# Attention and routed experts on one core: the next batch's scale of v five steps later, its loads, maxima and splits later too, z's splits four steps later, and another rate for the weights' work

## The chip, the cores and the metric

The program runs on one core of a Trainium2 chip. TensorE (PE in the profile) multiplies matrices, VectorE (DVE) and ScalarE (ACT) do elementwise work, GpSimd (POOL) issues scattered transfers, SyncE (SP) issues nearly all other transfers. The metric is device time in microseconds (us), the median of the runs of a kernel. Run to run it spreads by some 0.3% (2160.58 to 2166.72 us before the change).

## What is computed

The reference, cut to what matters (B = 8 batches, S = 2496 tokens, D = 256, d_qk = 64; 8 experts with F = 1024):

```python
scores = (1/S) * z @ z.T                    # per batch, S x S
attn   = maximum(scores, 0) ** 2
x      = u * (attn @ v)                     # (B*S, D) rows
xn     = x / norm(x);  en = emb / norm(emb)
idx    = argmax(xn @ en.T / tau);  gate = softmax(...)[idx]
out    = gate * (maximum(x @ w1[idx], 0) @ w2[idx])
```

The kernel multiplies in float16 and keeps float32 precision by halves: it splits every operand into a high and a low float16 part, scaled by a power of two that is found on the chip: for z, v and each expert's weights it takes the largest absolute value, turns it into a power of two, and then writes the two halves.

## The kernel before, in words

**Two phases.** In the first some 1315 us the attention of the 8 batches runs, with the routing of the rows of x and the splitting of the experts' weights beside it; then come the experts' products. The change touches the first phase alone.

**Steps.** The first phase is a loop over 800 steps (line 1085 on): batch b, group g of 512 query tokens (5 groups, 0 to 4; the last has 448), and 20 key tiles of 128 tokens. A step is written here by its number within its batch, 0 to 99, so steps 60 to 79 are group 3 and 80 to 99 the last group. In each step PE does `values` (lines 373 to 393: 12 products, into `acc`). Scores are symmetric: a tile is computed once (`scores`, lines 279 and 280; ACT makes relu and square, lines 283 and 284; `parts` makes high and low halves `hl` on DVE, lines 326 and 327) and for later groups turned by a DMA transpose on SP (lines 340, 342). So only "own" steps compute scores: 20 in group 0, then 16, 12, 8 and 4. In group 3 these are the steps 72 to 79; steps 60 to 71 have `values` alone. `scores` runs three own steps ahead of its use.

**Preparing the next batch.** `ahead(b)` makes a list of (step, flag, work) for batch b + 1, and the loop takes from its head what is due: loads and maxima of z (`scan_load`, `scan_max`), then of v (ten tiles `vr`, line 107; maxima line 121), the scale of z in steps 54 and 58, the scale of v in steps 64 and 68, then the loads (`z_load`, line 181), the splits (`z_split`: ACT line 192, DVE line 195) and copies (`z_copy`) of z. An item whose flag is set waits while `state["pm"]` holds, and with it all behind it in the list.

**A scale** has two pieces (`scale_pieces`). `across` reduces the maxima on DVE (line 132, `smv`), lets PE transpose the column (line 134, into `pm`) and reduces again on DVE (lines 136, 137, 139, `smbv`). `spread` lets PE spread the result over the partitions (line 144, into `pm`) and makes the scale on DVE (lines 146, 148). `pm` is one single buffer (pool `psM`), shared with the rank of the routing and the scales of the weights.

**Routing.** After each group `route` makes a queue of 29 small works, one taken per step. Those of the group before run in the next one: squares on ACT (line 445), a root on DVE (lines 713 to 727), a split of the rows (ACT line 468, DVE line 469) and its DMA transpose (line 472). The rank (lines 524, 525 on PE, into `pm`) comes in step 3 of the next but one group and is read in step 5 (`place`, lines 534, 537, 539, `pos`); between the two `state["pm"]` holds. In the steps of a batch this is 63 to 65, so v's `across` of step 64 runs in step 66.

**Splits of v** (`v_split`, ACT line 243, DVE line 244) are written in the program for steps 78 and 79 (`early = 2`) and 80 to 97. **Weights**: 22 works per expert (`wq`: loads lines 585 and 588, maxima line 596, scales lines 602 to 617, splits lines 645 and 646), one taken whenever `wsum`, which grows by `WRATE` per step, passes 1.

**Order.** PE executes in the order of the program, so a product that waits stops PE. For DVE, ACT and SP a scheduler sets the order when the kernel is built; each then executes in that order.

Of the kernel before, what the change touches and what calls it, by code (L numbers as in the profile page):

```python
# [43 lines left out]
def relu2_attention_then_moe(ctx, tc, zT, u, v, emb, tau, w1, w2, ident, tri, iota_e, out):  # L44
# [40 lines left out]
    NVP = NST // 2  # L85
# [17 lines left out]
    def scan_load(b, what, i, eng=None):  # L103

        if what == "v":
            t = vring.tile([P, 2, D], F32, name="vr", tag="vv")
            (eng or nc.sync).dma_start(t, v[b, 2 * i * P:2 * (i + 1) * P, :].rearrange("(j p) d -> p j d", p=P))
            for j in range(2):
                vraw[b, 2 * i + j] = t[:, j, :]
            scan[b, what, i] = t.rearrange("p j d -> p (j d)")  # L110
            return
        t = wk.tile([P, SCAN], F32, name="scan", tag="scan", bufs=1)
        src = zT[b, i * (DQ // ZSCANS):(i + 1) * (DQ // ZSCANS), :]
        (eng or nc.sync).dma_start(t, src.rearrange("a c -> (a c)").rearrange("(p w) -> p w", p=P))
        scan[b, what, i] = t

    def scan_max(b, what, i):
        if i == 0:
            n = (NVP if b else NV0) if what == "v" else ZSCANS if b else 3
            scan[b, what] = sml.tile([P, n], F32, name="smx" + what)  # L120
        nc.vector.tensor_reduce(scan[b, what][:, i:i + 1], scan.pop((b, what, i)), axis=AX.X, op=ALU.max,
                                apply_absolute_value=True)
# [48 lines left out]
    def z_tiles(b):  # L171
        Zs[b] = (zpool.tile([P, SP], F16, name="z1", tag="z1"),
                 zpool.tile([P, SP], F16, name="z2", tag="z2"))
# [3 lines left out]
    def z_load(b, c0):  # L177
        zt = zpool.tile([P, ZC], F32, name="zt", tag="zt", bufs=3)
        c1 = min(c0 + ZC, SP)
        m = P if b == 0 else DQ  # L180
        nc.sync.dma_start(zt[:m, :c1 - c0], zT[b, :m, c0:c1])
        zraw[b, c0] = zt

    def z_split(b, c0):
        zt = zraw.pop((b, c0))
        w = min(ZC, SP - c0)
        c1 = c0 + w
        z1, z2 = Zs[b]
        c = slice(c0, c1)
        lo, hi = slice(0, DQ), slice(DQ, P)  # L190
        k = scan[b, "cz"]
        hi_ = nc.scalar.activation(z1[lo, c], zt[lo, :w], AF.Copy, scale=k[lo]).ins
        if b == 0:
            nc.scalar.activation(z2[hi, c], zt[hi, :w], AF.Copy, scale=k[hi])
        lo_ = nc.vector.scalar_tensor_tensor(z2[lo, c], zt[lo, :w], k[lo], z1[lo, c], op0=ALU.mult, op1=ALU.subtract).ins
        if b:
            state["as"], state["ds"] = hi_, lo_
        if b == 0:
            nc.vector.scalar_tensor_tensor(z1[hi, c], zt[hi, :w], k[hi], z2[hi, c], op0=ALU.mult, op1=ALU.subtract)  # L199

    def z_copy(b, c0, c1):
        z1, z2 = Zs[b]
        c = slice(c0, c1)
        nc.sync.dma_start(z1[DQ:P, c], z2[0:DQ, c])
        nc.sync.dma_start(z2[DQ:P, c], z1[0:DQ, c])
# [549 lines left out]
    accs = {}  # L755
    wq = [f for e in range(E) for f in weights(e)]
    wsum = 0.0
    WRATE = {False: (0.0, 0.18, 0.22, 0.37, 0.33), True: (0.2, 0.3, 0.3, 0.35, 0.35)}

# [283 lines left out]


    NB = NG * NST
    early = 2

    def ahead(b):  # L1050

        todo = []
        for i in range(ZSCANS):
            todo.append((16 + 8 * i, False, lambda i=i: scan_load(b + 1, "z", i)))
            todo.append((23 + 8 * i, False, lambda i=i: scan_max(b + 1, "z", i)))
        for i in range(NVP):
            todo.append((3 * i + 25, False, lambda i=i: scan_load(b + 1, "v", i)))
            todo.append((3 * i + 34, False, lambda i=i: scan_max(b + 1, "v", i)))
        at = {"z": 54, "v": 3 * NVP + 34}
        for k, what in enumerate("zv"):  # L1060
            for j, f in enumerate(scale_pieces(b + 1, what)):
                todo.append((at[what] + 4 * j, True, f))
        at = 64
        gap = 2
        todo.append((0, False, lambda: z_tiles(b + 1)))
        for k in range(ZN):
            todo.append((max(0, at + (k - 3) * gap), False, lambda k=k: z_load(b + 1, k * ZC)))
            todo.append((at + k * gap, False, lambda k=k: z_split(b + 1, k * ZC)))
            if k in (ZN // 2, ZN - 1):
                c0, c1 = (0, (k + 1) * ZC) if k == ZN // 2 else ((ZN // 2 + 1) * ZC, SP)  # L1070
                todo.append((at + k * gap, False, lambda c0=c0, c1=c1: z_copy(b + 1, c0, c1)))
        return sorted(todo, key=lambda x: x[0])

    todo = []
    nd = 0
    for i, (b, g, q, s) in enumerate(steps):
# [10 lines left out]
        if q == 0:  # L1087
            accs[b, g] = [psA.tile([P, 512], F32, name=f"acc{k}", tag=f"a{2 * ((b * NG + g) % 2) + k}") for k in range(2)]
            nx = (b, g + 1) if g + 1 < NG else (b + 1, 0)
            upiece = None  # L1090
            if nx[0] < B:
                uts[nx], upiece = u_load(*nx)
            if g == 0 and b + 1 < B:
                todo = ahead(b)
# [51 lines left out]
        if i >= NST + 6:  # L1146
            wsum += WRATE[b == B - 1][g]
        if wsum >= 1 and not state["pm"]:
# [116 lines left out]
```

## Time and profile before

| | before |
|---|---|
| runs, us | 2160.58, 2164.53, 2166.72 (median 2164.53) |
| the profiled execution, us | 2163.31 |
| its span in the trace, us | 2161.7 |
| granted TensorE clock, mean | 0.992 |
| PE / DVE / ACT busy, us | 2102.2 / 1326.1 / 1026.0 |

A span is the time from the first to the last instruction in the trace; the profiled execution's own time has 1.6 us more. PE is busy 97% of the span, so what can be won without taking products away lies in PE's waits and in the clock that it is granted. The views used below are: who waited for whom, busy time by stretch, and the instructions in order of time.

### The profile page before, as it was taken

What the parts mean: (1) busy time and instruction counts of PE and PEld (TensorE: products, weight loads), DVE (VectorE), ACT (ScalarE), POOL (GpSimd) and SP (SyncE); (2) the same over time, 40 slices, a digit from 0 to 9 for tenths busy, and PEclk for the clock granted to TensorE, in tenths of its full rate; (3) what the DMA queues carried; (4) which work ended last, traced back from release to release, by engine and by line L of the source; (5) the groups of instructions that cost most, each with busy time, mean ns of one, the idle gap of its engine ahead of it and who ended that gap; (6) DMA issues with size and microseconds to landing.
All of it is one profiled execution on the core that took longest, in us unless ns stands there. A gap on an engine that the chain in (4) does not pass through costs nothing. (4 is left out here: it accounts for less than half of the span.)

```text
span 2161.7 us, 50676 instructions
## 1 busy us (share of the span) xinstructions
PE 2102.2 (97%) x19210; PEld 1789.3 (83%) x19210; DVE 1326.1 (61%) x4005; ACT 1026.0 (47%) x2131; POOL 328.5 (15%) x344
## 2 busy tenths in 40 slices
PE   6999999999999999999999999999999999999998
PEld 4878878878878878878778888888888888888888
DVE  8787787787787787787787874433333333333333
ACT  7676666566666566666566652222222222222211
POOL 0011011011011011011011102211211111211111
PEclk9999999999999999999999999999999999999999
DMA  6977977977977987977987968433323332257474
GB/s 160 193 157 157 195 164 153 192 169 150 205 162 152 188 176 152 199 165 153 197 166 165 184 134 205 124 71 89 92 55 92 89 89 50 50 135 198 131 201 115
DMA packets 661832, 317.60 MB, mean 147 GB/s; under 512 B 562885, under 2 KB 639310, under 8 KB 655440
## 3 DMA queue, kind: packets, MB, share of 16 engines
q1 hardware_dynamic: 646112, 272.76, 59.9%
q0 software_dynamic: 15184, 41.24, 6.9%
q8 instruction: 152, 2.49, 0.5%
q14 instruction: 96, 0.79, 0.1%
q10 hardware_dynamic: 288, 0.33, 0.1%
HBM read 255.11 MB, written 59.60 MB: 146 GB/s over the span
## 5 line engine op out<-in xcount | busy, mean ns | idle before, releaser
L283 ACT ACTIVATE a<-sc 128x512 f32<-128x512 f32 (+1 forms) x480 | 269.7, 562 | 271.7 <-PE sc L280 208.8
L548 POOL DMA_INDIRECT xs<-row,dsti x160 | 168.2, 1051 | 1016.0 <-ACT a L283 442.2
L284 ACT ACTIVATE a<-a 128x512 f32<-128x512 f32 (+1 forms) x480 | 285.9, 596 | 11.2
L384 PE MATMUL acc<-vv,tt 128*128 128x256 f16 x1152 | 273.9, 276 | 0.0
L386 PE MATMUL acc<-vv,tt 128*128 128x256 f16 x1152 | 273.7, 276 | 0.0
L1011 POOL DMA_INDIRECT out_dram<-ot,me x159 | 154.6, 972 | 662.5 <-DVE ot L1010 638.6
L1006 PE MATMUL po<-w,hl 128*128 128x256 f16 x928 | 252.9, 273 | 0.0
L1004 PE MATMUL po<-w,hh 128*128 128x256 f16 x928 | 252.9, 273 | 0.0
L1005 PE MATMUL po<-w,hh 128*128 128x256 f16 x928 | 252.9, 273 | 0.0
L1010 DVE TENSOR_SCALAR ot<-po,me,w 128x256 f32<-128x256 f32 x116 | 58.3, 540 | 216.4 <-PE po L1006 212.5
L388 PE MATMUL acc<-vv,tt 128*128 128x256 f16 x1152 | 181.2, 276 | 0.0
L279 PE MATMUL sc<-z 128*128 128x512 f16 (+1 forms) x480 | 175.8, 366 | 4.2 <-DVE z L199 4.1
L280 PE MATMUL sc<-z,z 128*128 128x512 f16 (+1 forms) x480 | 175.8, 366 | 0.0
L1006 PEld LDWEIGHTS <-hl 128*128 128x128 f16 x1272 | 124.5, 98 | 14.4
L1005 PEld LDWEIGHTS <-hh 128*128 128x128 f16 x1272 | 124.5, 98 | 14.2
L1004 PEld LDWEIGHTS <-hh 128*128 128x128 f16 x1272 | 124.5, 98 | 14.2
L388 PEld LDWEIGHTS <-tt 128*128 128x128 f16 x1152 | 114.1, 99 | 14.3
L386 PEld LDWEIGHTS <-tt 128*128 128x128 f16 x1152 | 114.1, 99 | 14.0
L384 PEld LDWEIGHTS <-tt 128*128 128x128 f16 x1152 | 113.9, 99 | 14.1
L468 ACT ACTIVATE row<-x,up 128x256 f16<-128x256 f32 x160 | 70.9, 497 | 69.4 <-DVE up L456 64.4
L1004 PE MATMUL po<-wb,hh 128*128 128x256 f16 x344 | 93.8, 273 | 0.0
L1005 PE MATMUL po<-wb,hh 128*128 128x256 f16 x344 | 93.8, 273 | 0.0
(5250 smaller groups left out, 5493.9 us busy)
## 6 DMA issues: line engine op xcount, KB each, us to landing
w<-wsd SPq DMA_DIRECT2D x64, 1026.0 KB
wa<-wsd SPq DMA_DIRECT2D x46, 1024.0 KB
w<-wsd SPq DMA_DIRECT2D x42, 1024.0 KB
wb<-wsd SPq DMA_DIRECT2D x24, 1026.0 KB
ut<-in_u_dram SPq DMA_DIRECT2D x72, 256.0 KB
vr<-in_v_dram SPq DMA_DIRECT2D x70, 256.0 KB
wr<-in_w_dram SPq DMA_DIRECT2D x64, 256.0 KB
wsd<-wo SPq DMA_DIRECT2D x64, 256.0 KB
```

The costliest lines, as they stand in the source:

```text
L279: nc.tensor.matmul(sc[:, :n], z1[:, ss], z1[:, t0:t0 + n], start=True, stop=False)
L280: nc.tensor.matmul(sc[:, :n], z1[:, ss], z2[:, t0:t0 + n], start=False, stop=True)
L283: state["at"] = nc.scalar.activation(a[:, :n], sc[:, :n], AF.Relu, scale=2.0 ** -SHIFT).ins
L284: nc.scalar.activation(a[:, :n], a[:, :n], AF.Square)
L384: nc.tensor.matmul(outs[j], piece(ph, j), vh, start=first and j % 2 == 0, stop=False, skip_group_check=True)
L386: nc.tensor.matmul(outs[j], piece(ph, j), vl, start=False, stop=False, skip_group_check=True)
L388: nc.tensor.matmul(outs[j], piece(pl, j), vl if last else vh, start=False, stop=ends, skip_group_check=True)
L548: put = nc.gpsimd.indirect_dma_start(xs[:, :], bass.IndirectOffsetOnAxis(ap=loc["dsti"][:m, j:j + 1], axis=0), row[:m, j, :], None)
L1004: nc.tensor.matmul(o, hh[:, f, t], wh, start=(f == 0), stop=False)
L1005: nc.tensor.matmul(o, hh[:, f, t], wl, start=False, stop=False)
L1006: nc.tensor.matmul(o, hl[:, f, t], wh, start=False, stop=(f == NF - 1))
L1011: put = nc.gpsimd.indirect_dma_start(out, bass.IndirectOffsetOnAxis(ap=me.bitcast(U32)[:, j, 1:2], axis=0), ot[:, j, :], None, bounds_chec ...
```

## The change

Seven numbers change. The scale of v goes from steps 64 and 68 (in effect 66 and 68) to 71 and 75. The loads of v go from steps 25 to 52 to 28 to 55, its maxima from 34 to 61 to 37 to 64. The splits of z go from 64 to 82 to 68 to 86, with their loads (58 to 76 to 62 to 80) and copies (74 and 82 to 78 and 86). The splits of v are written for steps 80 to 99. The weights' rates by group change from 0, 0.18, 0.22, 0.37, 0.33 to 0.05, 0.2, 0.28, 0.28, 0.29 (both 22 works in 100 steps). No instruction is added or removed.

```diff
-    WRATE = {False: (0.0, 0.18, 0.22, 0.37, 0.33), True: (0.2, 0.3, 0.3, 0.35, 0.35)}
+    WRATE = {False: (0.05, 0.2, 0.28, 0.28, 0.29), True: (0.2, 0.3, 0.3, 0.35, 0.35)}
...
-    early = 2
+    early = 0
...
-            todo.append((3 * i + 25, False, lambda i=i: scan_load(b + 1, "v", i)))
-            todo.append((3 * i + 34, False, lambda i=i: scan_max(b + 1, "v", i)))
-        at = {"z": 54, "v": 3 * NVP + 34}
+            todo.append((3 * i + 28, False, lambda i=i: scan_load(b + 1, "v", i)))
+            todo.append((3 * i + 37, False, lambda i=i: scan_max(b + 1, "v", i)))
+        at = {"z": 54, "v": 3 * NVP + 41}
...
-        at = 64
+        at = 68
```

**ACT, batch 1, from the end of group 2 to step 72.** Before the change ACT's order is (`a` relu and square of scores, `sq` the routing's squares, `row` its row splits, `z_2878` a split of z, `vv` a split of v):

```order
L507 ACTIVATE ex<-sh 128x32
L283 ACTIVATE a<-sc 128x512
L192 ACTIVATE z_2878<-zt,scz 64x256
L284 ACTIVATE a<-a 128x512
L445 ACTIVATE sq,n_4495<-x 128x256 x4
L192 ACTIVATE z_2878<-zt,scz 64x256
L468 ACTIVATE row_100<-x,up 128x256 x2
L192 ACTIVATE z_2878<-zt,scz 64x256
L468 ACTIVATE row_100<-x,up 128x256 x2
L192 ACTIVATE z_2878<-zt,scz 64x256
L243 ACTIVATE vv<-vr,scv 128x256 x15
L283 ACTIVATE a<-sc 128x512
```

After the change, the same place:

```order
L507 ACTIVATE ex<-sh 128x32
L283 ACTIVATE a<-sc 128x512
L284 ACTIVATE a<-a 128x512
L445 ACTIVATE sq,n_4496<-x 128x256 x4
L192 ACTIVATE z_2875<-zt,scz 64x256
L468 ACTIVATE row_100<-x,up 128x256 x3
L192 ACTIVATE z_2875<-zt,scz 64x256
L468 ACTIVATE row_100<-x,up 128x256
L283 ACTIVATE a<-sc 128x512
```

The first split of z now stands behind the four squares instead of ahead of them, and the run of 15 splits of v ahead of step 72's scores is gone.

**ACT, batch 1, steps 75 to 78, after the change.** Here the splits of v now begin, two at a time between the scores' works:

```order
L284 ACTIVATE a<-a 128x256
L243 ACTIVATE vv<-vr,scv 128x256 x2
L283 ACTIVATE a<-sc 128x256
L192 ACTIVATE z_2875<-zt,scz 64x256
L284 ACTIVATE a<-a 128x256
L243 ACTIVATE vv<-vr,scv 128x256 x2
L239 ACTIVATE vh<-vr,scv 64x256
L283 ACTIVATE a<-sc 128x448
```

Six of the 20 splits stand ahead of the end of group 3, the other 14 in the last group.

**DVE, batch 1, the second half of v's `across`.** Before (`smbv` is what PE's spread waits for; `z_2879` the low half of z, `row_100` of a row, `mx` a weights' maximum):

```order
L195 SCALAR_TENSOR_TENSOR z_2879<-zt,scz,z_2878 64x256
L724 SCALAR_TENSOR_TENSOR xy<-xt_4636,xy 128x4
L469 SCALAR_TENSOR_TENSOR row_100<-x,up,row_100 128x256
L727 TENSOR_TENSOR xs<-xn2c,xy 128x4
L596 TENSOR_REDUCE mx<-wr_3760 128x1
L136 TENSOR_REDUCE sm1v<-pm 1x1
L460 TENSOR_SCALAR inv<-xs,ceps 128x4
L137 TENSOR_SCALAR sm1v<-sm1v 1x1
L461 RECIPROCAL inv<-inv 128x4
L139 TENSOR_SCALAR smbv<-sm1v 1x1
```

After:

```order
L727 TENSOR_TENSOR xs<-xn2c,xy 128x4
L460 TENSOR_SCALAR inv<-xs,ceps 128x4
L461 RECIPROCAL inv<-inv 128x4
L462 SCALAR_TENSOR_TENSOR inv<-inv,itau,dn 128x4
L136 TENSOR_REDUCE sm1v<-pm 1x1
L137 TENSOR_SCALAR sm1v<-sm1v 1x1
L139 TENSOR_SCALAR smbv<-sm1v 1x1
L195 SCALAR_TENSOR_TENSOR z_2876<-zt,scz,z_2875 64x256
L326 CAST hl__4786<-a 128x4x128
L326 CAST hl__4809<-a 128x4x128
```

The chain from `pm` to `smbv` now stands behind the whole root of the routing and ahead of the first halves `hl` of group 3's own steps.

## Rows read from the trace of the kernel before

**Rows 1.** The page: span, and busy time, share and instructions of each engine.
```profile
span 2161.7 us, 50676 instructions
PE 2102.2 (97%) x19210; PEld 1789.3 (83%) x19210; DVE 1326.1 (61%) x4005; ACT 1026.0 (47%) x2131; POOL 328.5 (15%) x344
```
**Rows 2.** Waits of PE, 100 to 1160 us: who, for whom; us, times, longest.
```profile
PE pm L134 <- DVE pos L539: 12.7, 6, 3.3
PE pm L144 <- DVE smbv L139: 7.9, 5, 1.9
PE acc L384 <- DVE hl__16713 L326: 1.7, 1, 1.7
...
PE acc L384 <- DVE hl__15359 L326: 0.4, 1, 0.4
...
PE acc L384 <- DVE hl__2239 L326: 0.4, 1, 0.4
```
**Rows 3.** Busy time by stretch: batch 1's groups 2, 3, 4; batch 7's group 3.
```profile
core 0: us, PE busy (x) PEld busy (x) DVE busy (x) ACT busy (x) POOL busy (x), PEclk, DMA share, GB/s
255.00:287.00 32.00, 32.00 (x289) 26.36 (x287) 26.49 (x91) 17.77 (x39) 4.35 (x4) 1.00 1.06 231
...
287.00:324.00 37.00, 33.36 (x281) 26.91 (x280) 29.53 (x110) 23.91 (x60) 4.21 (x5) 0.91 0.60 132
...
324.00:351.00 27.00, 27.00 (x255) 23.19 (x253) 17.12 (x69) 12.79 (x29) 4.67 (x5) 1.00 0.61 132
...
1260.00:1289.00 29.00, 29.00 (x274) 25.04 (x272) 18.70 (x64) 16.07 (x38) 3.89 (x4) 1.00 0.73 160
```
**Rows 4.** The same view, stretches behind v's scale, batches 1, 2, 3, 6.
```profile
298.00:306.00 8.00, 7.29 (x40) 5.34 (x41) 6.01 (x30) 2.63 (x8) 3.90 (x4) 0.59 0.71 186
462.00:470.00 8.00, 7.46 (x41) 5.40 (x42) 5.91 (x31) 2.53 (x7) 3.88 (x4) 0.60 0.66 173
622.00:633.00 11.00, 8.24 (x58) 6.58 (x59) 9.92 (x42) 6.56 (x17) 3.89 (x4) 0.84 0.68 169
...
1108.00:1118.00 10.00, 7.71 (x53) 6.09 (x54) 8.96 (x38) 5.73 (x15) 3.89 (x4) 0.83 0.61 159
```
**Rows 5.** PE in order of time, batch 1: start, us, instruction [idle before <-releaser].
```profile
293.62 0.60 PE L388 MATMUL acc<-vv,tt 128*128 128x256 f16 x4
...
294.93 0.60 PE L388 MATMUL acc<-vv,tt 128*128 128x256 f16 x4
298.71 0.37 PE L134 MATMUL pm<-idt,smv 128*1 128x128 f32 x1 [3.19 <-DVE pos L539]
...
300.58 1.06 PE L388 MATMUL acc<-vv,tt 128*128 128x256 f16 x4
```
**Rows 6.** SP's issues in order of time, batch 1.
```profile
289.74 0.58 SPq L181 DMA_DIRECT2D zt<-in_zT_dram  x1
290.43 1.22 SPq L342 DMA_TRANSPOSE joint<-hl__4462  x1
```
**Rows 7.** ACT in order of time, batch 1.
```profile
291.94 0.51 ACT L192 ACTIVATE z<-zt,scz 64x256 f16<-64x256 f32 x1 [4.95 <-DMA zt<-in_zT_dram]
...
297.16 0.91 ACT L468 ACTIVATE row<-x,up 128x256 f16<-128x256 f32 x2 [1.30 <-DVE up L456]
...
305.14 6.11 ACT L243 ACTIVATE vv<-vr,scv 128x256 f16<-128x256 f32 x15 [5.00 <-DVE scv L148]
```
**Rows 8.** DVE in order of time, batch 1.
```profile
295.01 0.17 DVE L713 TENSOR_SCALAR xn2c<-n 128x4 f32<-128x4 f32 x1 [4.46 <-ACT sq L445]
295.09 0.68 DVE L596 TENSOR_REDUCE mx<-wr 128x1 f32<-128x512 f32 x1
...
298.53 0.19 DVE L539 TENSOR_TENSOR pos<-pos,ob 128x32 f32<-128x32 f32 x1
```
**Rows 9.** Waits of ACT, 100 to 1160 us.
```profile
ACT z L192 <- DMA zt<-in_zT_dram: 35.5, 21, 5.2
```
**Rows 10.** PE in order of time, batch 0: the spread of z's scale, step 58.
```profile
125.14 0.38 PE L144 MATMUL pm<-smbz,ones_f 1*128 1x1 f32 x2
```

## The prediction

> **What bounds the kernel now.** I read the page first: PE is busy 2102.2 of 2161.7 us [rows 1], so the change can win only what PE waits or what it runs at the lower clock. Next the waits of PE between 100 and 1160 us, which leave out the start and batch 7. Two lines stand out, and both belong to the scale of v: the transpose (line 134) waits 12.7 us in six batches, for `pos`, the last step of the routing's `place`; the spread (line 144) waits 7.9 us in five, for `smbv` [rows 2]. The other lines are waits of `values` for a half `hl`, 0.4 to 1.7 us each. Then the busy time by stretch: group 3 of batch 1, where v's scale is made, takes 37 us at a mean clock of 0.91; group 3 of batch 7, where no next batch is prepared, 29 us at 1.00 [rows 3]. So the place to look at is group 3 of batches 0 to 6.
>
> **Why PE waits there.** Three rows of batch 1 give the chain. ACT stands idle 4.95 us until 291.94, for the load of z's first piece [rows 7], which SP issued only at 289.74 [rows 6]; by ACT's order the routing's squares stand behind that split. DVE waits 4.46 us for the squares and begins the root at 295.01 [rows 8]. `pos` stands on DVE behind two splits of z, most of the root and two weights' maxima and ends at 298.7 [rows 8]. PE came to the transpose at 295.5 (the step's last products begin at 294.93 and last 0.60) and waits 3.19 us [rows 5]. It isn't a case of batch 1 alone: ACT waits 35.5 us for z's loads, 21 times [rows 9].
>
> Behind such a wait PE gets the lower clock: the same four products take 0.60 us before it and 1.06 us after it [rows 5]. The granted clock shows 0.59 of 8 us, 0.60 of 8, 0.84 of 11 and 0.83 of 10 in four batches [rows 4], that is 1.2 instead of 2.4 GHz for a part of each stretch. At 1.00 as much work would take 8 x 0.41 + 8 x 0.40 + 11 x 0.16 + 10 x 0.17 = 9.9 us less.
>
> The Trainium skill (TensorE: Matmul & The Clock Gate, Part 1, the caveats on the trace of the clock gate) says that recorded clock events are not to be trusted singly and should be checked against what the matmuls cost; were the records wrong, the 9.9 us would not be there to be won and the sum below would end at 2142. The doubled 1.06 us [rows 5] decides for the records.
>
> **The change part by part.**
>
> *v's scale to steps 71 and 75.* What goes: 12.7 + 7.9 + 9.9 = 30.5 us, if PE finds `pos` and `smbv` ready. For the transpose: it moves from two steps behind the rank to seven behind it. A step without scores takes 1.31 us (293.62 to 294.93 [rows 5]); without the wait PE in batch 1 would start step 66 at 295.5 and come to the new place at 295.5 + 5 x 1.31 = 302.0. `pos` is ready earlier, an estimate from rows: the squares no longer stand behind z's first split, but the load of that split now stands behind two turns `joint` on SP (1.22 each [rows 6]) and is issued near 293; it took 2.2 us from issue to ACT (289.74 to 291.94 [rows 6, 7]), so the split runs near 295.2, then three row splits at about 0.45 (0.91 for two [rows 7]), then `pos`: about 298. Cover: 4 us. If that cover is gone, each us late costs 1 us per batch and perhaps the clock again. For the spread: it follows four steps later, about 6 us with scores in three of them. DVE's chain lines 136 to 139 stands behind nothing that is still open once the root is done, so it needs 1 us of these 6. What stays: the instructions themselves. What they cost beside full work is seen with z's scale, whose spread runs in 0.38 us with no wait ahead of it [rows 10]; between 100 and 1160 us no wait of z's scale is in the list at all [rows 2]. I take 30.5, the whole; the bounds are 30.5 and half of it, 15 (below).
>
> Who waits behind the moved instructions: on DVE the reads of the spread (lines 146, 148) now stand between the halves `hl` of steps 75 and 76, and behind them ACT's first split of v, behind that the scores of step 76. No wait of this kind at this place is in the trace. Its nearest rows: the waits of `values` for `hl`, 0.4 to 1.7 us [rows 2]; so 0 to 7 x 1.7 = 12 us. I take 0, as z's scale, likewise among own steps (12 in group 2), has none [rows 2], and as `values` begins with the high half alone.
>
> *v's splits (`early` 0).* The order shows the real move: a run of 15 splits that keeps ACT from 305.14 to 311.25 [rows 7], ahead of step 72's scores, dissolves into pairs, and 14 go to the last group. The late start behind that run leaves five waits of 0.4 us for `hl` (first and last of them in rows 2): 2.0 us, of which I take 1. In the last group 14 x 0.41 (6.11 / 15 [rows 7]) = 5.7 us are added to ACT and about as much to DVE, which have 27 - 12.79 = 14.2 and 27 - 17.12 = 9.9 us to spare there [rows 3], and 16 of its 20 steps need nothing of them. Cost nothing; without that cover PE would wait in the last four steps.
>
> *z's splits, loads and copies four steps later.* Four splits then lie in the last group instead of two: 1 us more on either engine, in the same spare time. The first use is the next batch's scores in step 97; the second copy moves from step 82 to 86, 11 steps or some 14 us ahead. Nothing.
>
> *v's loads and maxima three steps later.* On SP they pass some of the rows' turns and of the weights' loads; the last maximum is due in step 64, seven steps or 9 us ahead of the scale. Nothing.
>
> *The weights' rate.* 22 works per batch before and after. Group 2 gets 1.2 more, at 0.68 us for a maximum [rows 8]: 0.8 us on a DVE with 26.49 busy of 32 [rows 3]. Group 3 gets 1.8 fewer. Group 2 is where DVE has least room: at worst one wait like the 1.7 [rows 2] in every batch, 12 us; at best group 1's and 2's waits go, some 6 us. I take nothing.
>
> **The sum.** Against the profiled execution: 2163.3 - 30.5 - 1 = 2131.8, rounded 2132 us. The median of the runs before is 1.2 us above that execution, well inside their spread of 6 us; I give 2132 for the median after.
>
> **The rivals.**
>
> *The wait comes along.* `pos` or `smbv` is still late in steps 71 and 75, since the load of z that ACT waits for comes later too. For it: the same chain, with 35.5 us of such waits [rows 9], and only 4 us of cover. Against it: five more steps, and the squares first. Half of the 30.5 stays: 2147 (2139 to 2155).
>
> *The scores' chain pays.* In steps 73 to 79 DVE and ACT must serve scores, z's splits, v's scale and v's first splits at once, without the time that PE's waits gave them: group 3 shrinks from 37 to near 31 us with 29.5 us of DVE work in it [rows 3]. If every batch waits 1.7 us [rows 2] in two or three steps, 4.4 us in all, the gain is gone: 2163.
>
> *Slower: v's splits hold up the hand-over.* A split's buffer is free only once PE has left an older tile of v in the last group; on ACT, behind the waiting split, stand z's last split, the row splits and the relus of step 96 on. DVE spares 9.9 us there, of which the added 5.7 and 1.0 leave 3.2. To end above 2170 the hand-over must cost (2170 - 2132) / 7 = 5.4 us per batch, so these queues must stand still 8.6 us; with 9.6 the time is 2177. Against it: PE leaves those tiles in steps 82 to 86, ten steps ahead of 96.
>
> *More than the sum.* Group 1's and 2's waits go as well: 2126.
>
> That the change doesn't do what it says is excluded by the orders shown.
>
> **How the numbers follow.** Forecast 2132 (2128 to 2138): 0.73. The wait comes along: 0.13. More: 0.05. The scores' chain pays: 0.05. Slower: 0.04. For faster by over 0.3% (6.5 us, about what a measurement of this kernel can tell from no change) count the first three: 0.91; same 0.05, slower 0.04. The range takes the forecast, the better case down to 2125 and the rival's nearer half up to 2145.
>
> **What would show it.** Right: in the waits of PE between 100 and 1130 us the lines `pm L134 <- pos` and `pm L144 <- smbv` are gone or under 1 us in all; the clock is 1.00 through group 3 of every batch; group 3 of batch 1 takes about 31.5 us; ACT's squares run ahead of its wait for z. Wrong: `pm L134` waits under another name (`smv`, `pos`), or `acc L384 <- hl` grows by more than 5 us, in group 3 for the scores' chain, at the end of group 4 for the hand-over. The forecast fails above all if z's first load lands over 4 us later than I worked out.

## The result, and the profile after

The changed kernel takes 2133.9 us (median; 2132.47 to 2135.95) against 2162.56 us for the kernel before in the same comparison, a ratio of 0.9873 with a 95% interval of 0.9859 to 0.9888. The forecast was 2132, its range 2125 to 2145. The profiled execution has 2132.47 us and this page:

```profile
span 2130.9 us, 50630 instructions
...
PE 2091.0 (98%) x19210; PEld 1785.8 (84%) x19210; DVE 1316.9 (62%) x4005; ACT 1024.0 (48%) x2131; POOL 376.5 (18%) x344
```

Against [rows 1] the span is 30.8 us shorter, with the same number of products; the 46 instructions fewer are none of PE, DVE, ACT or POOL, whose counts are the same. PE's waits between 100 and 1130 us after the change (engine, tile and line, whom it waited for; us in all, times, longest):

```profile
PE acc L384 <- DVE hl__14087 L326: 1.7, 1, 1.7
PE acc L384 <- DVE hl__16711 L326: 1.6, 1, 1.6
PE acc L384 <- DVE hl__11463 L326: 1.5, 1, 1.5
...
PE acc L384 <- DVE hl__12092 L326: 0.5, 1, 0.5
```

Both lines at the head of [rows 2], the transpose 12.7 us and the spread 7.9, are gone without a rest. What is left are waits for `hl`, all in step 27 but the 0.5 us; those of step 27 are 7.7 us where they were 5.0. (Steps are counted here by the products of `values` from the start of a batch, from 0; the expectations call this one step 26.) Group 3 by stretch, first the whole of it in batch 1, then the places that answer to [rows 4]:

```profile
285.20:315.40 30.20, 30.20 (x282) 25.75 (x280) 21.07 (x87) 17.04 (x43) 3.83 (x4) 1.00 0.76 150
...
296.00:304.00 8.00, 8.00 (x72) 6.76 (x70) 5.03 (x25) 2.71 (x6) 3.83 (x4) 1.00 0.80 154
454.00:462.00 8.00, 8.00 (x70) 6.57 (x69) 3.70 (x12) 2.74 (x5) 3.61 (x4) 1.00 0.62 137
```

PE is busy for all 30.20 us (second column) and the granted clock is 1.00. In [rows 3] the same group took 37.00 us at 0.91.

To see where the time went, I took from both traces the start of each group's first product of `values`; the products are the same, so a difference of two durations is waits and clock:

| us | before | after | difference |
|---|---|---|---|
| group 3, batches 0 to 6 | 33.0, 37.2, 37.3, 35.4, 34.7, 34.0, 35.3 (247.0) | 30.2 each (211.3) | -35.6 |
| group 1, all batches | | | +3.9 |
| group 2, all batches | | | -1.1 |
| batch 7, groups 3 and 4, to the start of its last step | | | +3.2 |
| all else (the experts' products above all) | | | -1.2 |
| span | 2161.7 | 2130.9 | -30.8 |

So group 3 gave more than the 31.5 us of the sum, and the rest gave 4.8 of it back. The experiments ask which part of the change did which.

### The profile page after: what moved, and what is told of

It reads as the page before. It is cut to its first block, busy times and chain, and to the rows that moved or that the text cites. A ratio compares the mean times of both kernels' runs of the same rounds, so it can differ in the third digit from the quotient of the medians.

```text
span 2130.9 us, 50630 instructions
## 1 busy us (share of the span) xinstructions
PE 2091.0 (98%) x19210; PEld 1785.8 (84%) x19210; DVE 1316.9 (62%) x4005; ACT 1024.0 (48%) x2131; POOL 376.5 (18%) x344
## 5 line engine op out<-in xcount | busy, mean ns | idle before, releaser
L548 POOL DMA_INDIRECT xs<-row,dsti x160 | 216.1, 1350 | 970.6 <-ACT a L283 427.6
L384 PE MATMUL acc<-vv,tt 128*128 128x256 f16 x1152 | 268.9, 273 | 0.0
L386 PE MATMUL acc<-vv,tt 128*128 128x256 f16 x1152 | 268.8, 273 | 0.0
L388 PE MATMUL acc<-vv,tt 128*128 128x256 f16 x1152 | 178.0, 273 | 0.0
L1006 PEld LDWEIGHTS <-hl 128*128 128x128 f16 x1272 | 124.4, 98 | 14.5
L388 PEld LDWEIGHTS <-tt 128*128 128x128 f16 x1152 | 112.6, 98 | 13.1
L384 PEld LDWEIGHTS <-tt 128*128 128x128 f16 x1152 | 112.5, 98 | 13.0
L386 PEld LDWEIGHTS <-tt 128*128 128x128 f16 x1152 | 112.6, 98 | 12.8
```

The costliest lines, as they stand in the source:

```text
L384: nc.tensor.matmul(outs[j], piece(ph, j), vh, start=first and j % 2 == 0, stop=False, skip_group_check=True)
L386: nc.tensor.matmul(outs[j], piece(ph, j), vl, start=False, stop=False, skip_group_check=True)
L388: nc.tensor.matmul(outs[j], piece(pl, j), vl if last else vh, start=False, stop=ends, skip_group_check=True)
L548: put = nc.gpsimd.indirect_dma_start(xs[:, :], bass.IndirectOffsetOnAxis(ap=loc["dsti"][:m, j:j + 1], axis=0), row[:m, j, :], None)
L1006: nc.tensor.matmul(o, hl[:, f, t], wh, start=False, stop=(f == NF - 1))
```

## The experiments

All ratios are against runs of the kernel before in the same comparison (medians 2160.9 to 2163.7); a difference between two comparisons carries the spread of both.

**The two halves apart: the scale alone (e1), z's splits alone (e2).**

```diff
 e1: before, with
-        at = {"z": 54, "v": 3 * NVP + 34}
+        at = {"z": 54, "v": 3 * NVP + 41}
 e2: before, with
-        at = 64
+        at = 68
```

> The kernel before with the scale of v alone moved, to steps 71 and 75. Distance theory (the waits came because v's scale stood two steps behind the read of the rank; five steps more are enough whatever ACT does): the waits of PE for pos and smbv and the lower clock behind them go, 28 to 31 us, so 2132 to 2135 and a ratio of 0.986 to 0.987, though the first split of z still stands ahead of the squares on ACT and ACT still waits some 35 us for its loads. Rival (the moved splits and loads of z are needed as well, since the root of the routing still starts 4.5 us late): half of the waits stays under other names, pm L134 or acc L384 <- hl, and the time is 2142 to 2155.

> The kernel before with z's splits, loads and copies alone four steps later; v's scale stays in steps 66 and 68. The squares now stand ahead of z's first split on ACT. Chain theory (PE waited only because DVE stood 4.5 us for the squares): the root of batch 1 starts near 290.5 instead of 295.0, pos is ready near 294.2, before PE comes at 295.5; the 12.7 us for pos go, most of the 7.9 for smbv and the clock too, and the time is 2133 to 2145. Distance theory (two steps behind the rank are too few even for a root in time): pm L134 keeps half of its 12.7 or more, pm L144 its 7.9, and the time is 2150 to 2160.

The scale alone: 2129.2 us, 0.9835 [0.9808, 0.9862], the whole gain. PE's waits from 100 to 1130 us in e1, all of them:

```profile
PE acc L384 <- DVE hl__14089 L326: 1.6, 1, 1.6
PE acc L384 <- DVE hl__16713 L326: 1.1, 1, 1.1
PE acc L384 <- DVE hl__11465 L326: 0.7, 1, 0.7
PE acc L384 <- DVE hl__8841 L326: 0.5, 1, 0.5
```

No transpose, no spread, and no `hl` wait in group 3 either: that takes 30.2 us in each of the seven batches, as in the full change, though ACT still stands 5.12 us for z's load ahead of the squares in batch 1.

z's splits alone: 2154.8 us, 0.9952 [0.9933, 0.9970]. The waits of e2 at the two lines, then DVE of e2 in batch 1 in order of time (start, length, line, instruction, [idle before it and who ended that]):

```profile
PE pm L134 <- DVE pos L539: 13.5, 6, 3.1
PE pm L144 <- DVE smbv L139: 1.6, 6, 0.4
...
PE pm L134 <- DVE carry L537: 0.9, 1, 0.9
```
```profile
288.44 0.17 DVE L713 TENSOR_SCALAR xn2c<-n 128x4 f32<-128x4 f32 x1
...
293.25 0.69 DVE L596 TENSOR_REDUCE mx<-wr 128x1 f32<-128x512 f32 x1 [3.06 <-DMA wr<-in_w_dram]
...
295.66 0.48 DVE L195 SCALAR_TENSOR_TENSOR z<-zt,scz,z 64x256 f16<-64x256 f32 x1 [0.72 <-ACT z L192]
...
296.27 0.19 DVE L539 TENSOR_TENSOR pos<-pos,ob 128x32 f32<-128x32 f32 x1
```

This is the instructive one. The squares are in time and the root begins at 288.44 instead of 295.01 [rows 8]. By the chain that I read in the trace of before, `pos` would then be ready ahead of PE. It isn't, for two loads still stand ahead of it on DVE. A weights' maximum waits 3.06 us for its own load. Behind that the low half of z waits 0.72 us more for ACT's split, which had stood 3.86 us for z's load, moved along with the split. `pos` ends at 296.46. The low half of z is the last thing that DVE waited for ahead of `pos` in six of the seven batches (0.2 to 2.1 us), the weights' maximum in batch 4. So squares in time are not enough, and the chain theory, by which e2 gains some 18 us or more, falls; z's load itself is not cleared by e2.

The wait for `pos` is 13.5 us where it was 12.7, with 0.9 for `carry`, which stands just ahead of it; only the spread's went, from 7.9 to 1.6. Most of the 9 us that e2 gains is clock. Taking one minus the granted clock, times the length of group 3, over batches 0 to 6, the lower clock cost 10.2 us in the kernel before (batches 1, 2, 3 and 6, at 0.91, 0.91, 0.95 and 0.95) and 1.7 in e2 (batch 6, at 0.95).

**All but the scale (e6).**

```diff
 e6: after, with
-        at = {"z": 54, "v": 3 * NVP + 41}
+        at = {"z": 54, "v": 3 * NVP + 34}
```

> The changed kernel with v's scale back in steps 64 and 68 and all else as changed. It tells what the later place of the scale gives once the rest is done. Distance theory: 2150 to 2160, waits of PE for pos and smbv back at two thirds of the 20.6 us or more. Chain theory: 2134 to 2145, since the squares stand ahead of z's split here too. If v's later loads and maxima make the scale late by themselves (the last maximum is due in step 64, the scale too), pm L134 waits under the name smv.

2164.3 us, 0.9995 [0.9976, 1.0014]: nothing gained, less than either theory expected. Its waits at the transpose, and ACT in batch 4, where the longest (3.87 us) is:

```profile
PE pm L134 <- DVE pos L539: 16.2, 5, 3.9
PE pm L134 <- DVE carry L537: 3.4, 2, 3.2
```
```profile
780.87 0.51 ACT L192 ACTIVATE z<-zt,scz 64x256 f16<-64x256 f32 x1 [5.78 <-DMA zt<-in_zT_dram]
```
```profile
781.41 0.48 DVE L195 SCALAR_TENSOR_TENSOR z<-zt,scz,z 64x256 f16<-64x256 f32 x1 [4.04 <-ACT z L192]
```

The second line is DVE's: its low half of z stands 4.04 us behind ACT's split, and `pos` (784.09) behind that. It is z's load again, now between the squares and `pos`, and so it is in all seven batches of e6 (DVE waits 1.2 to 4.1 us). In e6 the order of ACT has the 15 splits of v in one run although `early` is 0, and step 76's wait for `hl` is there; in e1, with `early` 2, it isn't. That run is dissolved by the later scale, not by `early`.

**Loads out of the way (e10).** If late loads ahead of `pos` make the wait, taking them away must take the wait, with the scale left where it was:

```diff
 e10: before, with
-            todo.append((3 * i + 25, False, lambda i=i: scan_load(b + 1, "v", i)))
+            todo.append((3 * i + 21, False, lambda i=i: scan_load(b + 1, "v", i)))
...
-            todo.append((max(0, at + (k - 3) * gap), False, lambda k=k: z_load(b + 1, k * ZC)))
+            todo.append((max(0, at + (k - 3) * gap - (8 if k < 3 else 0)), False, lambda k=k: z_load(b + 1, k * ZC)))
...
-        if wsum >= 1 and not state["pm"]:
+        if wsum >= 1 and not state["pm"] and not (b < B - 1 and 55 <= i - b * NB < 66):
```

> The kernel before, v's scale still in steps 66 and 68, but without the loads that stood late ahead of pos: the first three loads of z eight steps sooner, the loads of v four steps sooner, and none of the weights' works in steps 55 to 65 (they follow from step 66 on). Queue theory (the distance was too small because DVE and ACT execute in order and some load always lands late ahead of pos: z's in the kernel before, a weights' load when z's were moved): DVE does not stand before pos, pos is ready before 295.5 in batch 1, the 12.7 us for pos fall under 4 and the time is 2135 to 2148 without moving the scale. Rival (DVE's own work ahead of pos is too much for two steps, loads or not): pm L134 keeps 8 us or more and the time is 2150 to 2162.

2188.2 us, 1.0131 [1.0104, 1.0158]: slower by 27 us, the time missed altogether. The waits at the two lines (the transpose is not in the list), and DVE in batch 1 behind `pos`:

```profile
PE pm L144 <- DVE smbv L139: 41.5, 7, 7.3
```
```profile
297.22 0.19 DVE L539 TENSOR_TENSOR pos<-pos,ob 128x32 f32<-128x32 f32 x1
...
301.91 0.69 DVE L596 TENSOR_REDUCE mx<-wr 128x1 f32<-128x512 f32 x1 [1.41 <-DMA wr<-in_w_dram]
...
305.87 0.69 DVE L596 TENSOR_REDUCE mx<-wr 128x1 f32<-128x512 f32 x1 [2.77 <-DMA wr<-in_w_dram]
306.47 0.13 DVE L139 TENSOR_SCALAR smbv<-sm1v 1x1 int32<-1x1 int32 x1
```

The mechanism shows twice. Without late loads ahead of it `pos` is ready 0.8 to 1.1 us before PE comes in all seven batches, and the 12.7 us are gone: DVE's own work ahead of `pos` fits into two steps. (That of the spread does not quite: in e2 and e4 DVE waits for nothing between the transpose and `smbv`, and PE still stands 0.2 to 0.4 us at the spread in six and five of the seven batches.) Since z's, v's and the weights' loads were moved at once, e10 does not say which of them would have been enough. And the weights' works that I held back came one behind the other from step 66 on; now in every batch two of their maxima that wait for loads stand ahead of `smbv`, the last link of the spread, and the 7.9 us became 41.5. The lower clock comes on top: 0.57 from 305 to 312 us, behind batch 1's spread. The Trainium skill (PSUM — Partial Sum Buffer, Engine vs sequencer instructions) calls the queues of VectorE and ScalarE strict FIFO; DVE's idle 2.77 us ahead of a maximum, with `smbv`'s last small instruction (line 139) behind it, agrees.

**How much distance is enough (e9).** With the old rate (below) the scale three steps sooner:

```diff
 e9: after with the old WRATE, and
-        at = {"z": 54, "v": 3 * NVP + 41}
+        at = {"z": 54, "v": 3 * NVP + 38}
```

> The changed kernel with the old rate and v's scale three steps sooner, in steps 68 and 72. It measures the cover. With the scale in 71, pos was ready 5.0, 4.2, 2.9, 4.5, 2.8, 3.7 and 4.5 us ahead of the transpose in batches 0 to 6; three steps of 1.31 us are 3.9. Distance theory: the transpose now waits some 1.0, 1.2 and 0.2 us in batches 2, 4 and 5 and not in the others, 1.5 to 4 us in all with little of the lower clock, and the time is 2128 to 2132. Rival (the own steps from 72 on, not the distance, are what made the later place good, or bad): waits of half the old 20.6 us come back, 2138 or more; or none at all and 2127.

2125.7 us, 0.9833 [0.9812, 0.9854], as good as step 71, and no wait at either line in the list. PE's transpose and DVE's `pos` in batch 2 of e9, the closest case:

```profile
449.69 0.27 PE L134 MATMUL pm<-idt,smv 128*1 128x128 f32 x1
```
```profile
449.50 0.19 DVE L539 TENSOR_TENSOR pos<-pos,ob 128x32 f32<-128x32 f32 x1
```

`pos` ends as PE begins; from batch 3 on, and in batch 0, it is 0.2 to 1.5 us ahead. By subtraction I had expected three waits of 0.2 to 1.2 us in batches 2, 4 and 5; PE stands 0.15 us in batch 2, 0.04 in batch 1 and not at all in the others. Six batches are within 0.9 us of the reckoned cover, batch 4 is 1.6 better. Step 66 was short by up to 3.3 us in the kernel before, step 68 just meets `pos`, step 71 has 2.6 to 6.3 us to spare in the changed kernel. Own steps at 72 do no harm.

**The weights' rate (e3, e4).**

```diff
 e3: after, with the rate of before; e4: before, with the rate of after
-    WRATE = {False: (0.05, 0.2, 0.28, 0.28, 0.29), True: (0.2, 0.3, 0.3, 0.35, 0.35)}
+    WRATE = {False: (0.0, 0.18, 0.22, 0.37, 0.33), True: (0.2, 0.3, 0.3, 0.35, 0.35)}
```

> The changed kernel with the weights' old rate by group. The changed kernel has 2.9 us more waits of values for hl in step 26 of group 1 than the one before, and 1.7 us more wait for a turned row in batch 7 with a clock dip behind it. If the new rate brings these (more works of the weights in groups 0 to 2): they go back to 4.9 us and the time is 2128 to 2131. If the rate is worth something itself (fewer works in group 3): hl waits appear in group 3 and it is 2136 to 2140. If it is worth nothing, as I put it in the sum: 2132 to 2136.

> The kernel before with the weights' new rate alone. Taking the new rate out of the changed kernel gained 6.7 us (2127.2 against 2133.9). Theory: the new rate costs this by itself, in two places that have nothing to do with v's scale, the halves hl of step 26 (some 3 us) and the wait for a turned row in step 97 of batch 7 with the lower clock behind it (some 3 us): 2167 to 2171 with the waits of PE for pos and smbv left at 18 to 23 us. Rival: the rate costs only beside the other parts, and alone it is worth nothing: 2161 to 2165.

e3 takes 2127.2 us, 0.9823 [0.9800, 0.9847]; e4 2167.2 us, 1.0026 [1.0010, 1.0043], with 18.2 us of waits left at the two lines of v's scale. Both ways the new rate costs 5 to 7 us. From the starts of the groups, group 1 is 6.2 us shorter in e3 than in the changed kernel over all batches, and batch 7's last group, to the start of its last step, 3.2. The first holds in every trace: group 1 takes 271.9 to 272.9 us with the new rate (the changed kernel, e4, e6) and 265.9 to 268.9 with the old (before, e1, e2, e3, e9, e10). The second is not so clear: 28.2 to 28.8 us with the new rate, but 25.4 to 28.5 with the old.

The new rate is no pure cost, either. In e4 no weights' maximum stands between the transpose and `smbv`, the spread's wait falls from 7.9 to 2.0 us, and group 3 of batches 0 to 6 is 6.9 us shorter than before (240.1). With the scale late nothing of this is left to win, and the cost alone shows. One place, batch 5: SP and DVE of the changed kernel ahead of step 27,

```profile
829.93 0.94 SPq L648 DMA_DIRECT2D wsd<-wo  x1
...
847.73 0.57 SPq L114 DMA_DIRECT2D scan<-in_zT_dram  x1
```
```profile
850.19 0.48 DVE L121 TENSOR_REDUCE smxz<-scan 128x1 f32<-128x320 f32 x1 [4.06 <-DMA scan<-in_zT_dram]
```

and of e3:

```profile
841.12 0.87 SPq L114 DMA_DIRECT2D scan<-in_zT_dram  x1
```
```profile
844.93 0.49 DVE L121 TENSOR_REDUCE smxz<-scan 128x1 f32<-128x320 f32 x1 [3.13 <-DMA scan<-in_zT_dram]
```

With 0.05 in group 0 a store of split weights (line 648) now falls among SP's transposes there; e3 has none in that group. z's load for the maxima is issued later behind it, DVE stands 4.06 us for it instead of 3.13, and the halves of step 27 wait behind DVE (1.7 against 0.9 us). DVE's wait for this load is the last ahead of step 27's `hl` in all six batches that wait there, 3.0 to 4.2 us in the changed kernel. That the store is the cause in every batch was not tried by itself.

**What is left: step 27 (c7) and step 97 (c8).** Both on the changed kernel with the old rate:

```diff
 c7
-            todo.append((16 + 8 * i, False, lambda i=i: scan_load(b + 1, "z", i)))
-            todo.append((23 + 8 * i, False, lambda i=i: scan_max(b + 1, "z", i)))
+            todo.append((16 + 9 * i, False, lambda i=i: scan_load(b + 1, "z", i)))
+            todo.append((25 + 9 * i, False, lambda i=i: scan_max(b + 1, "z", i)))
 c8
-        if KA >= XAHEAD and i == len(steps) - 1 - NST // 2:
+        if KA >= XAHEAD and i == len(steps) - 7:
```

> The changed kernel with the old rate, and z's loads for the maxima each nine steps apart instead of eight (from 16 on), their maxima nine steps behind the load instead of seven. What is left of PE's waits between 100 and 1130 us is step 26's wait for hl, behind DVE's wait for the first of these loads. If the maximum's place in DVE's order causes it, the 2.6 us there go and the time is 2124 to 2127; if the turned rows or the weights keep DVE late there, nothing changes, 2127 to 2129; if the later maxima make z's scale late, pm L134 waits under smz and it is 2130 or more.

> The changed kernel with the old rate, and the loads of the first expert's weights four steps later (behind step 93 of batch 7 instead of 89). SP's transpose of a row for step 97 stands behind transposes that take 5.3 and 3.2 us to issue while these loads run, against 1.2 elsewhere. If the loads stretch them, the 1.5 us wait in step 97 goes and the time is 2124 to 2127; if the products of the first expert then wait for their weights, it is given back or worse, 2128 to 2133.

c7: 2120.9 us, 0.9810 [0.9791, 0.9828], more than expected; between 100 and 1130 us PE waits nowhere. Two steps more between the load and its maximum are enough: it is the same fault as with v's scale, an instruction that waits for a load, ahead of `hl` in DVE's queue.

c8: 2122.4 us, 0.9815 [0.9797, 0.9833]; the wait of step 97 is gone. The changed kernel there: SP's issues in batch 7, PE's wait, and the stretch behind it:

```profile
1262.16 4.28 SPq L472 DMA_TRANSPOSE rowt<-row  x3
...
1269.53 5.31 SPq L937 DMA_TRANSPOSE xt<-xs  x1
...
1276.21 3.19 SPq L937 DMA_TRANSPOSE xt<-xs  x1
...
1280.13 1.21 SPq L472 DMA_TRANSPOSE rowt<-row  x1
```
```profile
1282.62 0.28 PE L480 MATMUL pt<-e,rowt 128*128 128x16 f16 x4 [3.64 <-DMA rowt<-row]
```
```profile
1282.00:1286.00 4.00, 3.38 (x20) 2.44 (x21) 1.82 (x11) 0.23 (x1) 0.00 (x0) 0.50 0.37 68
```

The last of four row turns is issued behind two slow transposes, PE waits 3.64 us, and its clock is 0.50 of full speed, 1.2 instead of 2.4 GHz, in the stretch that follows. In c8 the transposes still take 3.45 and 2.75 us:

```profile
1257.05 1.22 SPq L472 DMA_TRANSPOSE rowt<-row  x1
...
1258.95 4.63 SPq L472 DMA_TRANSPOSE rowt<-row  x3
...
1266.42 3.45 SPq L937 DMA_TRANSPOSE xt<-xs  x1
...
1271.48 2.75 SPq L937 DMA_TRANSPOSE xt<-xs  x1
```

so the wait went because all four row turns now stand ahead of them, not because they became quick.

**Together (b1, b2), and without z's and v's parts (e11).** b1 and b2 are one kernel: the changed one with the old rate and the edits of c7 and c8. e11 is the kernel before with three edits alone, e1's, c7's and c8's.

> The changed kernel with the old rate, z's loads for the maxima nine steps apart and the first expert's loads four steps later, the three edits that gained by themselves. c7 took the waits of step 26 (2120.9) and c8 that of step 97 (2122.4) from 2127.2. If they add up: 2114 to 2119, with no wait of PE left between 100 and 1280 us. If they overlap: 2119 to 2123.

> The kernel before with three edits alone: v's scale in 71 and 75, z's loads for the maxima nine steps apart, the first expert's loads four steps later. Against the best kernel so far (2118.8) it lacks only the later z splits, the later loads and maxima of v and the later splits of v. If these are worth nothing, as I put them in the sum: 2117 to 2121 and the same ratio within 0.002. If they spare waits once v's scale is late (DVE's queue in step 61 on is fuller with z's splits sooner): 2123 or more, with pm L134 or acc L384 back in the waits.

> The best kernel so far once more, beside the kernel with three edits alone on the same chip: 2116 to 2121, no wait of PE of 0.5 us or more between 100 and 1280 us.

b1 takes 2118.8 us, 0.9798 [0.9781, 0.9814]; beside each other e11 takes 2117.8 us, 0.9792 [0.9774, 0.9810], and b2 2117.0, 0.9790 [0.9774, 0.9805]. The later splits of z and v and the later loads of v are worth nothing that can be measured, once the scale is late. From 100 to 1280 us neither e11 nor b2 has a wait of PE in its list; b2 by stretch:

```profile
100.00:1250.00 1150.00, 1150.00 (x10353) 956.22 (x10351) 923.09 (x3164) 761.92 (x1653) 159.54 (x161) 1.00 0.85 177
```

PE is busy 1150.00 of 1150.00 us at the full clock. The first phase is at PE's bound there; both are some 16 us faster than the changed kernel. Against e3's median c7 gains 6.3 us and c8 4.8, both together 8 to 10. By the traces the two do not overlap: c7 takes 4.4 us out of group 1 and c8 1.7 out of batch 7's last group, and b2 has both; the rest is within the spread of the runs.

## Why the prediction was right, and where it was not

- **What bounds, and which wait ends last: right.** v's scale cost what the two lines said. The waits were 20.6 us in the sum and are 0.
- **The clock: right.** Group 3 became 35.6 us shorter. Of this 23.0 were idle time of PE and 10.2 lower clock by the granted clock over the whole group, where I took 9.9 from four stretches; 2.4 are neither, and what they are the runs don't show. Not each wait is followed by the lower clock: batches 0, 4 and 5 idle 2.4, 3.8 and 3.2 us in group 3 and read 1.00. (By the same terms group 3 of batch 1 should have been put at 30.3 us, 37.2 - 3.2 - 3.3 - 0.4, not at 31.5; it takes 30.2.) The caveat of the Trainium skill (TensorE: Matmul & The Clock Gate, Part 1) on recorded clock events did not decide here: what the records said was lost was really there to be won.
- **Why `pos` was late: half right.** The chain by z's load and the squares is one of several. e2 puts the squares first and `pos` is as late behind a weights' load and z's split; e6 behind z's split. What e10 shows is the general form: DVE executes in order, and some instruction that waits for a load stands ahead of `pos` in every order that was tried, except where the loads were moved. A run that moves z's first loads alone was not made, so how much is theirs stays open. I should have asked of each load-bound instruction ahead of `pos`, not of the first one that the chain named.
- **The cover: right, 1.3 us too large.** I had `pos` 10.6 us behind the start of group 3 and PE at the new place 14.6 behind it. In batch 1 of the changed kernel they stand 11.8 and 14.5 behind it. DVE there in order of time, then ACT and PE:

```profile
290.09 0.69 DVE L121 TENSOR_REDUCE smxv<-vr 128x1 f32<-128x512 f32 x1 [2.79 <-DMA vr<-in_v_dram]
...
290.89 0.16 DVE L713 TENSOR_SCALAR xn2c<-n 128x4 f32<-128x4 f32 x1
...
294.73 0.48 DVE L195 SCALAR_TENSOR_TENSOR z<-zt,scz,z 64x256 f16<-64x256 f32 x1 [2.08 <-ACT z L192]
...
296.82 0.19 DVE L539 TENSOR_TENSOR pos<-pos,ob 128x32 f32<-128x32 f32 x1
```
```profile
294.19 0.51 ACT L192 ACTIVATE z<-zt,scz 64x256 f16<-64x256 f32 x1 [6.17 <-DMA zt<-in_zT_dram]
```
```profile
299.28 0.60 PE L388 MATMUL acc<-vv,tt 128*128 128x256 f16 x4
299.71 0.27 PE L134 MATMUL pm<-idt,smv 128*1 128x128 f32 x1
```

   That leaves 2.7 us to spare instead of 4. ACT's split of z sets `pos`, as reckoned: the wait for it is DVE's last ahead of `pos` in all seven batches. In batch 1 it runs 9.0 us behind the start of the group where I had 7.8. A maximum of v, moved three steps later by the change and put at nothing in the sum, makes DVE wait 2.79 us ahead of the root, which begins at 290.89; by the order shown this cost nothing, for DVE then stands 2.08 us more for z.
- **v's splits: right in the time, wrong in the reason.** The `hl` waits of step 76 went wholly, with the shortest gaps 2.4 us of idle time where I took 1; but e1 and e6 show that the later scale dissolved the run of 15, not `early` 0. The 14 splits more in the last group hid as reckoned: group 4 of batches 0 to 6 is as long as before.
- **z's splits and v's loads: right.** e11 against b2: within 1 us.
- **The weights' rate: the term that was mis-sized.** I took 0 between -6 and +12 and named group 2 as the place. It cost 5 to 7 us (e3, e4), in group 1 ahead of step 27 and, not as surely, in batch 7's last group; the work more that group 0 got, and the 0.4 more of group 1, I had not priced at all. Its cost and the larger gain of group 3 nearly cancelled, so the total came out within 2 us of the median by more luck than its terms deserve.
- **The rivals.** The wait did not come along, the scores' chain asked nothing (group 3 has no wait left), and the hand-over held. "More than the sum", 2126, is near what the change gives with the old rate (e3, 2127.2), but by group 3, not by the waits of groups 1 and 2 that I had named.

## What to carry to other kernels

When PE waits for a small result of an in-order engine, list every instruction ahead of it there that waits for a load; moving one load to another place of the queue does not help while any other, or the same, still stands ahead, whereas moving the consumer some steps away covered them all. Distance is cheap here: two steps behind the rank were short by up to 3.3 us, four just enough, seven safe. Test the edits that ride along one by one; here one edit gave the whole gain and another gave 5 to 7 us of it back.

## What was not expected of the hardware

A transpose by DMA took SP 1.24 us to issue in the median of the changed kernel's first 1250 us, 2.8 at most, but 5.31 us in batch 7 where 1 MB loads of the first expert's weights are issued between the transposes. A row turn behind it in SP's order is issued that much later. The runs show the coincidence, and c8 that the turn's place decides whether PE pays; that the loads stretch the transposes wasn't shown by itself.
